# Attention outputs as two matmuls per block, one per head, summed by VectorE

## The chip, the cores and the metric

The kernel runs on one core of a Trainium2 chip. The metric is the device time of one execution in microseconds (us), the median over several runs. Besides the times there is one profiled execution, whose trace gives the start and the duration of every instruction on each engine.

## The reference

Attention over 8 batches, 8 heads, 576 positions and head size 64, in fp32, each query seeing 32 keys (heads 0 to 3: the last 32; heads 4 to 7: every fourth of the last 128). Behind it stands a gated feed-forward layer on the 4608 tokens.

```
scores = scale * q @ k^T, masked;  attn = softmax(scores);  x = attn @ v
xn  = x / sqrt(mean(x*x) + 1e-6) * rms_g
out = (silu(xn @ w_gate) * (xn @ w_val)) @ w_out        # 512 -> 1536 -> 512
```

## The kernel before

The tokens are cut into 16 units of 288. Heads go in pairs, four pairs c = 0 to 3 for each unit. A pair's queries are cut into blocks: three blocks of 96 queries for c < 2 (keys: 96 or 128 rows) and four blocks of 72 queries for c >= 2 (72 keys in even units, 104 in odd ones). That makes 14 blocks for a unit.

Products that need fp32 are made from two parts, a high one rounded to the type fp32r and a low one that is the rest; three of the four cross products are kept. In the feed-forward layer each product is three matmuls of 128x128 weights against 288 columns (`three`, lines 653 and 656). Attention does the same from the fourth unit on (u >= NEX = 3; the three units before use plain fp32).

Everything is issued by one hand-written schedule in slots. Slot after slot, the feed-forward layer of unit u takes, for j = 0 to 11, a gate slot (`gate`: 12 matmuls into `g`), a value slot (`val`, into `v`) and a projection slot (`proj` of the j before, into four accumulators `acc`). The attention of unit u+1 is fitted in between: behind the feed-forward matmuls of every second slot comes an attention event (`attend`, `products`). In the steady state an event holds, on TensorE in this order, the output matmuls of one block (o), two transposes of a later block's probabilities (t) and two score matmuls of a still later block (s). Events fall in turn on a projection, a value and a gate slot. In the text they are called P, V and G events. A unit has 36 slots: in 28 of them every second one has an event with scores, and the same holds for transposes and outputs, each shifted.

Work on the other engines is put off with `later(dt, rank, fn)`: it is issued dt slots later, sorted by rank, at the start of that slot (`flush`), before the slot's matmuls. Each engine runs its own instructions strictly in this order. For VectorE (DVE in the profile) the order behind an event in slot n is:

- behind a P event, slot n+1: `low_part` (line 469, at once behind ScalarE's copy `pt`, line 467), then `scores_max` (lines 379 and 384); slot n+2: `scores_norm` of an older block (404, 405), `add` (442), `silu` (698, reads `g` out of PSUM)
- behind a V event, slot n+1: `prod` (711, reads `v` out of PSUM), `scores_max`; slot n+2: `scores_norm`, `add`, `low_part`
- behind a G event, slot n+1: `silu`, `scores_max`; slot n+2: `low_part`, `scores_norm`, `add`, `prod`

PSUM has two banks, `g` and `v`, that gate and value products take in turn (`bank`). A projection slot's transposes, and those of a value slot in units from the fourth on, go into a tile of their own in bank `g` of the j that runs. So the transposes of a V event can start only when `silu` has read that bank; and the next gate product can start only when `prod` has read the value product. The outputs of an event have one bank, `o`.

For a block's outputs both heads' values stand side by side as 128 weight columns: `vhi` (ScalarE, line 319) and `vlo` (GpSimd, line 323). One matmul takes `vhi` against high and low probabilities of both heads (line 500: 4 x 96 or 4 x 72 columns), one takes `vlo` against the high ones (line 501), into the same place. Of each result only the half of the rows that belongs to the head is used. `take` (ScalarE, line 431) copies the low probabilities' part to `xraw`, and one slot later `add` (VectorE, line 442) adds the other part out of PSUM.

Of the kernel before, what the change touches and what calls it, by code (L numbers as in the profile page):

```python
# [11 lines left out]
F32R = mybir.dt.float32r  # L12
U32 = mybir.dt.uint32
AF = mybir.ActivationFunctionType
ALU = mybir.AluOpType
PSUM = bass.MemoryType.PSUM

B, H, S, D = 8, 8, 576, 64
DM, FF = 512, 1536
NT = B * S  # L20
P = 128
# [3 lines left out]
DIL = 4  # L25
QB = 96
NC = DM // P
NJ = FF // P
NNAT = 2
NEX = 3  # L30
# [31 lines left out]
def geometry(u, c):  # L62


    half = u % 2
    if c < NC // 2:
        if half:
            return [(QB * i, QB * i, 0, P) for i in range(U // QB)], QB, U + W
        return [(QB * i, max(QB * i - W, 0), 0 if i else W, P if i else QB)
                for i in range(U // QB)], QB, U  # L70
    nq = U // DIL
    keys = nq + (W if half else 0)
    return [(nq * r, keys * r, 0 if half else W, keys) for r in range(DIL)], nq, keys * DIL
# [3 lines left out]
def attn_moe(ctx: ExitStack, tc: tile.TileContext, qk_in, v_in, w_gate, w_val, w_out, rms_g, outT):  # L77
# [4 lines left out]
    V, A, G, PE = nc.vector, nc.scalar, nc.gpsimd, nc.tensor  # L82
# [36 lines left out]
    def later(dt, rank, fn):  # L119
        put_off.setdefault(now[0] + dt, []).append((rank, fn))  # L120
# [134 lines left out]
    heads, vs, late = {}, {}, []  # L255
# [39 lines left out]
    def load_v(b):  # L295

        if b is not None and b[0] >= NNAT:
            u, c, i = b
            vt = sb.tile([P, 2, D], F32, tag="vt", name=f"vt_{u}_{c}_{i}", bufs=3)
            nc.sync.dma_start(out=vt.rearrange("p a d -> p (a d)"), in_=v_in[u, c][:, i * 2 * D:(i + 1) * 2 * D])  # L300
            vs[b] = vt

    def further(b, n):

        k = everything.index(b) + n
        return everything[k] if k < len(everything) else None
# [4 lines left out]
    vparts = {}  # L311

    def split_v(b, dt):
        k = everything.index(b) % 2

        def hi():
            if k not in vparts:
                vparts[k] = [late[0].tile([P, 2, D], F32R, name=f"v{p}_{k}", bufs=1) for p in ("hi", "lo")]
            A.copy(out=vparts[k][0], in_=vs[b])  # L319

        def lo():
            vh, vl = vparts[k]
            G.tensor_tensor(out=vl, in0=vs.pop(b), in1=vh, op=ALU.subtract)  # L323
            load_v(further(b, 3))

        later(dt, 3.3, hi)
        later(dt, 5.1, lo)

    def after(u, h, n):

        k = u * H + h + n
        return divmod(k, H) if k < NU * H else None
# [37 lines left out]
    st, xraw, xsq = {}, {}, {}  # L370
# [44 lines left out]
    def take(u, c, i, o):  # L415

        blocks, nq, _ = geometry(u, c)
        if (u, c) not in xraw:
            xraw[u, c] = sb.tile([P, U], F32, tag="xraw", name=f"xraw_{u}_{c}", bufs=NC)
        x = xraw[u, c]  # L420
        if c < NC // 2:
            to = x[:, QB * i:QB * i + nq]
        else:
            to = x.rearrange("p (j r) -> p r j", r=DIL)[:, i, :]
        copy = V.tensor_copy if i % 2 and u == 0 and c == NC - 1 else A.copy
        if u < NEX:
            for a in range(2):
                copy(out=to[a * D:(a + 1) * D], in_=o[a * D:(a + 1) * D, a * nq:(a + 1) * nq])
        else:
            for a in range(2):  # L430
                A.copy(out=to[a * D:(a + 1) * D], in_=o[a * D:(a + 1) * D, (2 + a) * nq:(3 + a) * nq])  # L431
        if i == len(blocks) - 1:
            dt = 1 if c != 1 or u < NEX else 4
            later(dt, 0.44 if u >= NEX and (now[0] + dt - ends) % 3 == 0 else 2.5 if u else 1.9, lambda: square(u, c))

    def add(u, c, i, o):
        _, nq, _ = geometry(u, c)
        x = xraw[u, c]
        to = x[:, QB * i:QB * i + nq] if c < NC // 2 else x.rearrange("p (j r) -> p r j", r=DIL)[:, i, :]
        for a in range(2):  # L440
            rows = slice(a * D, (a + 1) * D)
            V.tensor_tensor(out=to[rows], in0=o[rows, a * nq:(a + 1) * nq], in1=to[rows], op=ALU.add)  # L442

    def square(u, c):
        first = c == 0
# [10 lines left out]
    def bursts(u):  # L456
        return [(u, c, i) for c in range(NC) for i in range(len(geometry(u, c)[0]))]

    everything = [b for u in range(NU) for b in bursts(u)]
# [14 lines left out]
    def products(q, t, o, t_ps, s_tag="s", o_tag="o", wait=0):  # L474


        if q:
            s_ps = ps.tile([P, 512], F32, tag=s_tag, name=f"s_{q[0]}_{q[1]}_{q[2]}")
        if o:
            o_ps = ps.tile([P, 512], F32, tag=o_tag, name=f"o_{o[0]}_{o[1]}_{o[2]}")  # L480
            pt = st.pop(o)
        if t:
            p, _ = st.pop(t)
        def transposed(a):
            blocks, nq, _ = geometry(*t[:2])
            n = blocks[t[2]][3]
            PE.transpose(t_ps[:n, a * QB:a * QB + nq], p[:nq, a, :n], ident[:nq, :nq])  # L487

        def output(a):
            blocks, nq, _ = geometry(*o[:2])  # L490
            n = blocks[o[2]][3]
            if a:
                return
            out = o_ps[:, :2 * nq].rearrange("d (a q) -> d a q", a=2)
            if o[0] < NEX:
                PE.matmul(out, vs.pop(o)[:n].rearrange("k a d -> k (a d)"), pt[:n, 0, :, :nq], start=True, stop=True)
                return
            vh, vl = (part[:n].rearrange("k a d -> k (a d)") for part in vparts[everything.index(o) % 2])
            both = o_ps[:, :4 * nq].rearrange("d (t a q) -> d t a q", t=2, a=2)
            PE.matmul(both, vh, pt[:n, :, :, :nq], start=True, stop=False)  # L500
            PE.matmul(out, vl, pt[:n, 0, :, :nq], start=False, stop=True)  # L501

        def scored(a):
            blocks, nq, _ = geometry(*q[:2])
            qc, kc, _, n = blocks[q[2]]
            sv = s_ps[:QB].rearrange("q (a t k) -> q a t k", a=2, t=2)
            if q[0] < NEX:
                qk = heads[q[0], 2 * q[1] + a]
                PE.matmul(sv[:nq, a, 0, :n], qk[:, qc:qc + nq], qk[:, U + kc:U + kc + n], start=True, stop=True)  # L509
                return  # L510
            qs, ks = heads[q[0], 2 * q[1] + a]
            PE.matmul(sv[:nq, a, :, :n], qs[:, qc:qc + nq], ks[:, :, kc:kc + n], start=True, stop=True)  # L512

        order = ((t, transposed), (o, output), (q, scored))
        if t and t[0] >= NEX:
            order = ((o, output), (t, transposed), (q, scored))
        parts = [(b, fn, a) for b, fn in order for a in range(2)]
        for b, fn, a in parts:
            if b:
                fn(a)  # L520
        if t:
            later(1, 0.2, lambda: untranspose(t, t_ps, wait))
        if o:
            later(1, 0.5, lambda: take(*o, o_ps))
            if o[0] >= NEX:
                later(2, -0.3, lambda: add(*o, o_ps))
            if o[0] < NEX:
                later(1, 9, lambda: load_v(further(o, 3)))
            far = further(o, 2)
            if far and far[0] >= NEX:  # L530
                split_v(far, 8 if o[0] < NEX else 1)
        if q:
            later(1, 0.7, lambda: scores_max(*q, s_ps))
            later(2, 0.42 if wait == 1 else 2, lambda: scores_exp(*q))
            later(3 if q[0] < NNAT else 4, -1, lambda: scores_norm(*q))
            u, c, i = q
            nxt = after(u, 2 * c, 2)
            nb = len(geometry(u, c)[0])
            if u < NEX:
                if u == NNAT - 1 and c == NC - 1 and i == nb - 1:  # L540
                    for h in range(4):
                        later(1, 9, lambda h=h: load(NNAT, h))
                if u >= NNAT and i == nb - 1 and c < NC - 1:
                    for a in range(2):
                        later(1, 9, lambda a=a: load(*after(u, 2 * c + a, 4)))
                if u == NEX - 1 and c == NC - 1 and i == nb - 1:
                    for a in range(2):
                        later(3 + a, 9, lambda a=a: split(NEX, a, (1, 2, 2, 3), G, G))
            elif nxt and i == 0:
                split(*nxt, (1, 2, 2, 3), G, G)  # L550
                split(nxt[0], nxt[1] + 1, (2, 3, 3, 4) if c < NC - 1 else (1, 2, 3, 4), G, G)
# [274 lines left out]
    for u in range(NU):  # L826
        for j in range(NJ):
            for part in range(0 if u + j else 2, 3):
                t = 3 * (u * NJ + j) + part
# [95 lines left out]
```

## Time and profile before

| what | value |
|---|---|
| median of 3 runs | 1115.47 us (1114.78 to 1117.87) |
| the profiled execution | 1115.13 us, span 1113.3 us, granted TensorE clock 1.0 |
| TensorE busy | 1101.7 us, 99% of the span |
| VectorE busy | 671.8 us, 60% |
| ScalarE (ACT) busy | 708.8 us, 64% |
| GpSimd (POOL) busy | 673.2 us, 60% |
| DMA engines | 24.1% of the span in the main queue |

A row of the timeline reads: start in us from the beginning of the span, duration, engine, line of the kernel, operation, tile written and tiles read, shape and count (x2 when two like instructions are merged), and in brackets the idle time of the engine before it and what ended it. A row of the groups reads: line, engine, operation, shapes, count, then total busy us and the mean in ns of one, then idle time before. PE is TensorE's matmul, PEld its weight load. Matmuls overlap, so what one costs is read from the distance of two starts and not from its duration.

### The profile page before, as it was taken

How to read it: one execution, taken by the hardware profiler on the slowest of the kernel's cores; microseconds unless marked ns; L12 is line 12 of the kernel's file. 1: busy time of each engine (PE TensorE's matmuls, PEld its weight loads, DVE VectorE, ACT ScalarE, POOL GpSimd, SP SyncE). 2: the span in 40 equal slices, each digit the busy share in tenths (PEclk: the TensorE clock that was granted, in tenths of full speed). 3: DMA queues.
4: the chain of work that ended last, by engine and by line, in shares of the span. 5: the costliest groups of instructions: out<-in, count | busy, mean ns of one | idle time of the engine just before them, and what ended most of it. 6: DMA issues, size and time to landing. Idle time of an engine off the chain costs nothing.

```text
span 1113.3 us, 25463 instructions
## 1 busy us (share of the span) xinstructions
PE 1101.7 (99%) x8362; PEld 1077.5 (97%) x8362; DVE 671.8 (60%) x2734; ACT 708.8 (64%) x2579; POOL 673.2 (60%) x1154
## 2 busy tenths in 40 slices
PE   8899999999999999999999999999999999999998
PEld 6787999999999999999999999999999999999998
DVE  6989667656565565656656565665656656565312
ACT  7795676757576675767657576675757657575311
POOL 6423588656586675757657575675658657584211
PEclk9999999999999999999999999999999999999999
DMA  9665212212131131311212121131212212120000
GB/s 255 194 245 183 74 47 82 84 35 81 41 94 50 42 86 40 95 39 57 80 39 84 42 83 54 48 96 28 88 43 80 64 32 80 49 78 13 11 12 22
DMA packets 61543, 82.16 MB, mean 74 GB/s; under 512 B 7299, under 2 KB 41091, under 8 KB 61411
## 3 DMA queue, kind: packets, MB, share of 16 engines
q1 hardware_dynamic: 61410, 80.54, 24.1%
q8 instruction: 66, 1.08, 0.4%
q14 instruction: 67, 0.54, 0.2%
HBM read 71.08 MB, written 9.44 MB: 72 GB/s over the span
## 4 chain that ended last, share of the span: by engine, by line
PE 95%; DVE 1%; DMA 1%; ACT 1%; POOL 1%; issue 0%; SPq 0%; POOLq 0%; DVEq 0%; ACTq 0%
PE acc L656 17%; PE g L656 17%; PE v L656 17%; PE acc L653 9%; PE g L653 9%; PE v L653 9%; PE s L512 3%; PE o L500 2%; PE acc L650 2%; PE v L650 2%; PE g L650 2%; PE t L487 2%; PE o L501 1%; PE g L487 1%; DMA v<-in_v_dram 1%; PE s L509 1%
## 5 line engine op out<-in xcount | busy, mean ns | idle before, releaser
L723 POOL TENSOR_TENSOR hlo<-th,hhi 128x288 fp32r<-128x288 f32 x179 | 145.8, 814 | 185.2 <-ACT hhi L722 168.1
L656 PE MATMUL acc<-hhi,lo 128*128 128x288 f32 x720 | 212.7, 295 | 0.0
L698 DVE SCALAR_TENSOR_TENSOR th<-th,g 128x288 f32<-128x288 f32 x180 | 81.8, 454 | 212.5 <-ACT pt L467 130.6
L395 ACT ACTIVATE t<-t,sum 96x128 f32<-96x128 f32 (+3 forms) x448 | 165.3, 372 | 33.0 <-DVE sum L384 31.6
L656 PE MATMUL g<-xhi,lo 128*128 128x288 f32 x612 | 180.3, 295 | 0.0
L656 PE MATMUL v<-xhi,lo 128*128 128x288 f32 x612 | 180.2, 294 | 0.0
L693 ACT ACTIVATE th<-g 128x288 f32<-128x288 f32 x180 | 73.9, 410 | 151.4 <-PE g L487 57.7
L411 POOL TENSOR_SCALAR t<-t,sum 72x72 f32<-72x72 f32 (+3 forms) x414 | 149.9, 374 | 32.2 <-DVE sum L405 20.0
L323 POOL TENSOR_TENSOR vlo<-vt,vhi 128x128 fp32r<-128x128 f32 x182 | 84.2, 463 | 116.6 <-ACT vhi L319 113.5
L656 PEld LDWEIGHTS acc<-hhi,lo 128*128 128x128 f32 x720 | 135.4, 188 | 0.0
L722 ACT CAST hhi<-th 128x288 fp32r<-128x288 f32 x180 | 77.8, 432 | 85.3 <-DVE th L711 84.7
L442 DVE TENSOR_TENSOR xraw<-o,xraw 64x72 f32<-64x72 f32 (+1 forms) x364 | 97.2, 267 | 42.1 <-ACT xraw L431 38.6
L656 PEld LDWEIGHTS v<-xhi,lo 128*128 128x128 f32 x612 | 115.1, 188 | 0.0
L656 PEld LDWEIGHTS g<-xhi,lo 128*128 128x128 f32 x612 | 115.1, 188 | 0.0
L711 DVE TENSOR_TENSOR th<-th,v 128x288 f32<-128x288 f32 x180 | 81.0, 450 | 54.7 <-PE v L656 53.0
L653 PE MATMUL acc<-hhi,hi_o 128*128 128x288 f32 x360 | 109.0, 303 | 0.0
L653 PE MATMUL g<-xhi,hi_g 128*128 128x288 f32 x357 | 106.8, 299 | 0.0
L656 PE MATMUL acc<-hlo,hi_o 128*128 128x288 f32 x360 | 106.4, 296 | 0.0
L431 ACT COPY xraw<-o 64x72 f32<-64x72 f32 (+1 forms) x364 | 95.4, 262 | 9.8 <-PE o L501 7.7
L353 POOL TENSOR_TENSOR ks<-qk,ks 128x288 fp32r<-128x288 f32 (+2 forms) x104 | 93.3, 902 | 3.1
L656 PE MATMUL g<-xlo,hi_g 128*128 128x288 f32 x322 | 95.1, 295 | 0.0
L362 POOL TENSOR_TENSOR qs<-qk,qs 64x288 fp32r<-64x288 f32 x104 | 84.2, 809 | 14.7 <-ACT qs L357 7.8
(188 smaller groups left out, 3524.5 us busy)
## 6 DMA issues: line engine op xcount, KB each, us to landing
qk<-in_qk_dram SPq DMA_DIRECT2D x60, 288.0 KB, 2.8
vt<-in_v_dram SPq DMA_DIRECT2D x196, 64.0 KB, 1.9
qk<-in_qk_dram SPq DMA_DIRECT2D x30, 352.0 KB, 3.1
out_dram<-ot SPq DMA_DIRECT2D x64, 144.0 KB, 1.9
qk<-in_qk_dram SPq DMA_DIRECT2D x30, 304.0 KB, 2.8
raw<-in_w_gate_dram SPq DMA_DIRECT2D x12, 512.0 KB, 4.7
raw<-in_w_val_dram SPq DMA_DIRECT2D x12, 512.0 KB, 4.2
raw<-in_w_out_dram SPq DMA_DIRECT2D x12, 512.0 KB, 4.3
```

What stands on the lines that cost most here:

```text
L323: G.tensor_tensor(out=vl, in0=vs.pop(b), in1=vh, op=ALU.subtract)
L353: ek.tensor_tensor(out=ks[:, 1, :nkt], in0=kr, in1=ks[:, 0, :nkt], op=ALU.subtract)
L362: eq.tensor_tensor(out=qs[D:], in0=qr[D:], in1=qs[D:], op=ALU.subtract)
L395: A.activation(out=t[:nq, a, :n], in_=t[:nq, a, :n], func=AF.Exp, scale=-1.0, bias=sm[:nq, a, 0:1], accum_out=sm[:nq, a, 1:2] if u or i % ...
L411: (V if u == 0 and (c, i) > (NC - 1, 0) else G).tensor_scalar(out=t[:nq, a, :n], in0=t[:nq, a, :n], scalar1=sm[:nq, a, 3:4], scalar2=1.0, ...
L431: A.copy(out=to[a * D:(a + 1) * D], in_=o[a * D:(a + 1) * D, (2 + a) * nq:(3 + a) * nq])
L442: V.tensor_tensor(out=to[rows], in0=o[rows, a * nq:(a + 1) * nq], in1=to[rows], op=ALU.add)
L653: PE.matmul(out, wh[:, cc, :], xh, start=start, stop=False)
L656: PE.matmul(out, w[:, cc, :], v, start=False, stop=stop and k == 1)
L698: V.scalar_tensor_tensor(out=t, in0=t, scalar=1.0, in1=g, op0=ALU.add, op1=ALU.mult)
L711: V.tensor_tensor(out=t, in0=t, in1=v_ps[:, :U], op=ALU.mult)
L723: (V if (u, j) == (NU - 1, NJ - 1) else G).tensor_tensor(out=lo, in0=t, in1=hi, op=ALU.subtract)
```

## The change

From the fourth unit on a head's high and low values stand side by side as one weight of 128 columns. There is one matmul for each head, against that head's high and low probabilities (2 x 96 or 2 x 72 columns). Rows 0 to 63 of the result then hold the high values' products with both parts, rows 64 to 127 the low values' products. VectorE adds three of the four quarters: a `tensor_reduce` over the two parts of rows 0 to 63, written to `xraw`, and an add of rows 64 to 127's product with the high part. ScalarE's two copies and the separate `add` one slot later are gone; `take` keeps its slot, with rank 0.55 instead of 0.5, so all four VectorE instructions of a block stand behind `low_part` and ahead of `silu` and `scores_max` of that slot.

```diff
 def split_v(b, dt):  # hi(), lo()
-                vparts[k] = [late[0].tile([P, 2, D], F32R, name=f"v{p}_{k}", bufs=1) for p in ("hi", "lo")]
-            A.copy(out=vparts[k][0], in_=vs[b])
+                vparts[k] = late[0].tile([P, 2, 2, D], F32R, name=f"vhl_{k}", bufs=1)
+            A.copy(out=vparts[k][:, :, 0], in_=vs[b])
...
-            vh, vl = vparts[k]
-            G.tensor_tensor(out=vl, in0=vs.pop(b), in1=vh, op=ALU.subtract)
+            vp = vparts[k]
+            G.tensor_tensor(out=vp[:, :, 1], in0=vs.pop(b), in1=vp[:, :, 0], op=ALU.subtract)
...
 def take(u, c, i, o):
-                A.copy(out=to[a * D:(a + 1) * D], in_=o[a * D:(a + 1) * D, (2 + a) * nq:(3 + a) * nq])
+                ours, cols = to[a * D:(a + 1) * D], 2 * a * nq
+                V.tensor_reduce(out=ours, in_=o[:D, cols:cols + 2 * nq].rearrange("d (t q) -> d q t", t=2),
+                                axis=mybir.AxisListType.X, op=ALU.add)
+                V.tensor_tensor(out=ours, in0=o[D:, cols:cols + nq], in1=ours, op=ALU.add)
...
-    def add(u, c, i, o):
-        ...
-            V.tensor_tensor(out=to[rows], in0=o[rows, a * nq:(a + 1) * nq], in1=to[rows], op=ALU.add)
...
 def output(a):
-            PE.matmul(both, vh, pt[:n, :, :, :nq], start=True, stop=False)
-            PE.matmul(out, vl, pt[:n, 0, :, :nq], start=False, stop=True)
+            vp = vparts[everything.index(o) % 2]
+            PE.matmul(o_ps[:, 2 * a * nq:2 * (a + 1) * nq].rearrange("d (t q) -> d t q", t=2),
+                      vp[:n, a].rearrange("k t d -> k (t d)"), pt[:n, :, a, :nq], start=True, stop=True)
...
-            later(1, 0.5, lambda: take(*o, o_ps))
-            if o[0] >= NEX:
-                later(2, -0.3, lambda: add(*o, o_ps))
+            later(1, 0.5 if o[0] < NEX else 0.55, lambda: take(*o, o_ps))
```

More of the change, by code (lines that the diff above doesn't have):

```diff
@@ L434, in take @@
             later(dt, 0.44 if u >= NEX and (now[0] + dt - ends) % 3 == 0 else 2.5 if u else 1.9, lambda: square(u, c))
-    def add(u, c, i, o):
[L437 to L442, printed above, removed]
     def square(u, c):
@@ L491, in output @@
             n = blocks[o[2]][3]
-            if a:
-                return
-            out = o_ps[:, :2 * nq].rearrange("d (a q) -> d a q", a=2)
             if o[0] < NEX:
+                if a:
+                    return
+                out = o_ps[:, :2 * nq].rearrange("d (a q) -> d a q", a=2)
                 PE.matmul(out, vs.pop(o)[:n].rearrange("k a d -> k (a d)"), pt[:n, 0, :, :nq], start=True, stop=True)
                 return
[L498 to L501, printed above, removed]
+            vp = vparts[everything.index(o) % 2]
+            PE.matmul(o_ps[:, 2 * a * nq:2 * (a + 1) * nq].rearrange("d (t q) -> d t q", t=2),
+                      vp[:n, a].rearrange("k t d -> k (t d)"), pt[:n, :, a, :nq], start=True, stop=True)
         def scored(a):
```

## The prediction

> **What bounds the kernel now.** I read the page's busy shares first, then the chain that ended last, then starts in the timeline.
>
> ```profile
> span 1113.3 us, 25463 instructions
> PE 1101.7 (99%) x8362; PEld 1077.5 (97%) x8362; DVE 671.8 (60%) x2734; ACT 708.8 (64%) x2579; POOL 673.2 (60%) x1154
> ...
> PE 95%; DVE 1%; DMA 1%; ACT 1%; POOL 1%; issue 0%; SPq 0%; POOLq 0%; DVEq 0%; ACTq 0%
> ```
>
> TensorE is busy for 99% of the span and is 95% of the chain. So time taken off TensorE counts at once, as long as nobody makes it wait; time added to VectorE counts only where TensorE waits for it. VectorE's 60% says nothing of that: its work stands in a fixed order with deadlines, and I look at these.
>
> **TensorE's part.** Distances of starts give what a matmul costs. First an event that holds outputs alone, then the outputs of a block of 96 queries:
>
> ```profile
> 498.55 0.30 PE L500 MATMUL o<-pt,vhi 104*128 104x288 f32 x1
> 498.69 0.23 PE L501 MATMUL o<-pt,vlo 104*128 104x144 f32 x1
> 498.75 0.34 PE L653 MATMUL g<-xhi,hi_g 128*128 128x288 f32 x1
> 498.93 0.29 PE L656 MATMUL g<-spare,hi_g 128*128 128x288 f32 x1
> 499.06 0.30 PE L656 MATMUL g<-xhi,lo 128*128 128x288 f32 x1
> ...
> 457.60 0.34 PE L500 MATMUL o<-pt,vhi 128*128 128x384 f32 x1
> 457.77 0.25 PE L501 MATMUL o<-pt,vlo 128*128 128x192 f32 x1
> 457.86 0.33 PE L487 MATMUL t<-ident,t 96*128 96x96 f32 x2
> ```
>
> 288 columns cost 0.13 us (498.93 to 499.06), 384 cost 0.17, 192 cost 0.09, so about 0.46 ns for a column. Were that all, the new pair would cost twice the old second matmul: 0.09 less for a block of 96 queries, 0.07 less for one of 72 (144 columns, 498.69 to 498.75). But from the start at 498.69 to that of the second matmul behind it (498.93) pass 0.24 us, not 0.07 + 0.13. The 144-column matmul takes 0.11 us when 128 weight columns must be loaded behind it. So I read 0.11 as the least between two matmuls when the second one's weight has 128 columns. The weight loads' groups agree:
>
> ```profile
> L501 PEld LDWEIGHTS o<-pt,vlo 128*128 128x128 f32 x66 | 12.4, 188 | 0.0
> ...
> L501 PEld LDWEIGHTS o<-pt,vlo 72*128 72x128 f32 x48 | 9.1, 190 | 0.0
> ```
>
> A load of 128 columns takes 188 to 190 ns with 128 rows or 72, so the short key blocks get no cheaper loads. The change keeps two loads of 128 columns for a block, and its first matmul (192 or 144 columns, 0.09 or 0.07 us) is now too short to cover the second load. It costs 0.112 (the 0.24 less a spacing of 0.13, with the third decimal that many spacings give). The second new matmul has the old second one's columns and successor, so nothing changes there. What is saved is the old first matmul less 0.112: 0.177 - 0.112 = 0.065 us for the 78 blocks of 96 queries (13 units x 6), 0.133 - 0.112 = 0.021 for the 104 of 72. That is 5.1 + 2.2 = 7.3 us. The ends are nothing (less can't be: no column and no load is added) and the column count's 13.7 (78 x 0.088 + 104 x 0.066); I take 7.3, as the event of 498.55 has the same load behind the same columns.
>
> On the page "TensorE: Matmul & The Clock Gate", section "LDWEIGHTS (loading the stationary operand)", the Trainium skill speaks against the larger gain: a load takes its columns over 1.2 in ns, whatever the rows. For 128 columns that is 107 ns; the trace agrees with its 0.11. By the page the sum would be 78 x 0.070 + 104 x 0.026 = 8.2 us.
>
> **What else moves at no cost.** ScalarE loses two copies a block; it isn't on the chain, and its `pt` and `hhi` wait for others. The high and low values are written as 64-column pieces instead of whole rows, the same elements in the same places of both queues; DMAs and SP's order stay. `take` waits on VectorE for the second output matmul. Queued behind it are `silu` and `scores_max`; whoever waits for these is what follows.
>
> **VectorE's part.** How long are the four instructions?
>
> ```profile
> L403 DVE TENSOR_REDUCE sum<-t 72x2 f32<-72x144 f32 x4 | 1.2, 297 | 0.7 <-ACT t L395 0.7
> ...
> L403 DVE TENSOR_REDUCE sum<-t 96x2 f32<-96x192 f32 x2 | 0.7, 345 | 0.0
> ...
> 455.04 0.34 DVE L469 TENSOR_TENSOR pt<-t,pt 128x192 fp32r<-128x192 f32 x1
> 455.31 0.41 DVE L379 TENSOR_TENSOR t<-s,mask 96x256 f32<-96x256 f32 x1
> ...
> 456.36 0.17 DVE L405 RECIPROCAL sum<-sum 96x2 f32<-96x2 f32 x1
> 456.44 0.50 DVE L442 TENSOR_TENSOR xraw<-o,xraw 64x96 f32<-64x96 f32 x2
> 456.98 0.46 DVE L698 SCALAR_TENSOR_TENSOR th<-th,g 128x288 f32<-128x288 f32 x1
> ```
>
> The reduces read 192 or 144 elements, as these rows do (0.345 and 0.297 us, from SBUF and to two outputs; the new ones read PSUM and write 96 or 72). An add is 0.25 (half of 0.50); I add 0.03 where 72 queries are written with a stride. Independent instructions overlap: L379 starts 0.07 before L469 ends, L442 0.09 before L405 ends. Behind the adds nothing does: L698 starts 0.04 after them. An add also needs its reduce's result. So I give each step from the first add to the one behind the last a gap of 0.03: 0.35 + 0.03 + 0.26 + 0.02 + 0.35 + 0.03 + 0.26 + 0.03 = 1.33; with 72 queries 0.33 and 0.29 give about the same. I take 1.32 as the shift of what follows. Low end: a reduce as short as an add and no gaps, 1.0. High end: 0.06 more for a reduce of many short sums, as much as 60 elements more at the rate of these two rows ((0.345 - 0.297) over 48), 1.45.
>
> The Trainium skill, page "VectorE: DVE Perf Modes", section "Two Vector instructions with no wait between them", has a rule for the gaps: an instruction is held until the one before is done if an input or the output starts in another quadrant of 32 partitions than before. The trace agrees (the 0.04 at 456.98); by the rule every step of the new `take` behind its first reduce is held.
>
> Now the deadlines. Behind a P event VectorE's order becomes low part, four new ones, `scores_max`, norm, `silu`; the old adds went behind the norm. In the rows above (unit of 457.86) L379 moves from 455.31 to 456.63, L405 ends at 457.85 instead of 456.53, and `silu` may overlap it: 457.77 instead of 456.98, which is +0.79. It ends at 458.23. The V event's transposes (457.86) wait for that bank. They would come at 457.73, since the outputs of the P event and of this V event are 0.065 shorter each. With 0.04 for the handing over TensorE waits 0.54 us. The same place in other units and blocks:
>
> ```profile
> 523.32 0.45 DVE L698 SCALAR_TENSOR_TENSOR th<-th,g 128x288 f32<-128x288 f32 x1
> 524.48 0.33 PE L487 MATMUL t<-ident,t 96*96 96x96 f32 x2
> ...
> 479.85 0.45 DVE L698 SCALAR_TENSOR_TENSOR th<-th,g 128x288 f32<-128x288 f32 x1
> 480.62 0.29 PE L487 MATMUL t<-ident,t 72*104 72x72 f32 x2
> ...
> 545.98 0.46 DVE L698 SCALAR_TENSOR_TENSOR th<-th,g 128x288 f32<-128x288 f32 x1
> 546.94 0.23 PE L487 MATMUL t<-ident,t 72*72 72x72 f32 x1
> ...
> 468.21 0.45 DVE L698 SCALAR_TENSOR_TENSOR th<-th,g 128x288 f32<-128x288 f32 x1
> 469.38 0.29 PE L487 MATMUL t<-ident,t 72*104 72x72 f32 x2
> ```
>
> - first such V event, even units (524.48): margin 0.71 instead of 0.42, wait 0.25
> - third, odd units (480.62): +0.73 (the strided adds taken out are 0.06 longer), and 0.13 earlier by the G event (below); margin 0.32, events 0.04 shorter, 0.04 to hand over: wait 0.36. Even units (546.94), margin 0.50: 0.18
> - second, odd units (469.38): margin 0.72, +0.79, 0.13 earlier, 0.13 and 0.04 as at 457.86: 0.11; in even units, and at the other two V events of a unit, `silu` waits for ScalarE today, which covers the shift
>
> Behind a G event VectorE is idle today:
>
> ```profile
> 472.90 0.34 PE L500 MATMUL o<-pt,vhi 128*128 128x384 f32 x1
> ...
> 474.23 0.46 DVE L698 SCALAR_TENSOR_TENSOR th<-th,g 128x288 f32<-128x288 f32 x1 [2.43 <-ACT pt L467]
> ```
>
> The second output matmul ends 0.42 us behind the start of the first (457.60 to 457.77 + 0.25); 0.065 less and 0.04 for the handing over make 0.40. So the four run from 473.30 to 474.63, and `silu` is 0.40 late. The adds that stood ahead of `prod` are gone, 0.54 (456.44 to 456.98). `prod` comes about 0.13 earlier, and with it `hhi`, `pt` and the next low part. Behind V events nothing but `scores_max` and older work waits, and its bank is asked for two slots later.
>
> Sum of waits, 7 odd and 6 even units (the last odd one without the 0.36, since `silu` is done earlier where no next unit is scored): 7 x (0.54 + 0.11) + 6 x 0.36 + 6 x (0.25 + 0.18) = 9.3 us. Against 7.3 saved: +2.0. The profiled execution took 1115.13 us (1.8 more than its span), 0.34 below the median; 1115.13 + 2.0 = 1117.1.
>
> **The rivals.**
>
> *The new VectorE chain is shorter* (faster). Were the four 1.13 us (a reduce like an add, 0.25), each wait falls by 0.19 where it is that long: 7 x 0.35 + 6 x 0.17 + 6 x 0.06 = 3.8 us, and the time is 1115.1 - 7.3 + 3.8 = 1111.6; at 1.0 some 1.7 us of waits are left: 1109.5. For it: the rows of reduces are of two long sums, not 96 short ones. Against: 192 elements took 0.345.
>
> *`silu` behind P events decides* (slower). Each 0.1 us more in the four costs 32 waits, 3.2 us. It passes 0.3% from 0.04 us beyond my 1.33; at 1.45 the time is 1117.1 + 3.8 = 1120.9. For it: margins of 0.32 to 0.72. Against: nothing in the rows asks for longer reduces.
>
> *The second load hides after all* (columns alone count): 13.7 saved, but the deadlines come 0.05 to 0.09 earlier at 32 places, so waits are 11.3: 1112.7. Against: the 0.24 at 498.69.
>
> *The waits don't arise*, because low parts come sooner once ScalarE has less to do: 1115.1 - 7.3 = 1107.8. For it: two instructions less on ScalarE in each event. Against: its copies stood behind `pt`.
>
> **How the numbers follow.** A measurement of this kernel can tell about 0.3% (3.3 us) from no change. My sum stands (gain and waits about cancel, 1112 to 1119): 0.40, with the third rival in it. Shorter chain or no waits: 0.28. `silu` decides: 0.32. So faster 0.28, same 0.40, slower 0.32. The range takes in the ends of the take's length and leaves some of both tails: 1109 to 1122.
>
> **What would show it.** Right: in events the two output matmuls 0.11 apart; four VectorE instructions of some 1.3 us behind the low part; `silu` ending just before a V event's transposes, and there a gap of 0.2 to 0.5 us on TensorE three times in an odd unit, twice in an even one; some 144 us more on VectorE (182 blocks x (1.33 - 0.54)), and ScalarE's two copies a block gone. Wrong: outputs 0.09 or 0.07 apart, reduces well off 0.3 us, gaps elsewhere (gate products waiting for `prod`, scores for `scores_max`), or no gaps.

## The result

| | median us | ratio to the kernel before (95% interval) |
|---|---|---|
| before | 1115.24 (4 runs) | |
| after | 1121.93 (1121.88 to 1124.24, 4 runs) | 1.0058 [1.0046, 1.0070] |

The change makes the kernel 6.7 us slower. The forecast was 1117.1, +2.0 us.

The profiled execution of the kernel after took 1124.24 us. That is 2.3 us above the median, and it was already 2.7 us behind the kernel before where the changed units begin: its granted clock (the column PEclk, behind the five engines) was 0.95 and 0.94 in the first 60 us, where the kernel before had 1.00.

```profile
core 0: us, PE busy (x) PEld busy (x) DVE busy (x) ACT busy (x) POOL busy (x), PEclk, DMA share, GB/s
0.00:30.00 30.00, 24.75 (x144) 18.95 (x145) 19.69 (x106) 20.87 (x81) 19.58 (x53) 0.95 0.96 245
30.00:60.00 30.00, 27.86 (x139) 22.30 (x139) 27.68 (x81) 21.44 (x73) 12.83 (x14) 0.94 0.58 182
```

From the first changed unit (at 190 us) to the last slot the two traces differ by 5.7 us. That is what has to be explained; the rest of the 6.7 is not placed (the profiled execution ran 0.7 us longer behind its last instruction).

The page of the kernel after, busy shares and the chain that ended last:

```profile
PE 1105.5 (98%) x8362; PEld 1074.1 (96%) x8362; DVE 782.8 (70%) x3098; ACT 618.8 (55%) x2215; POOL 671.7 (60%) x1154
...
PE 76%; DVE 12%; ACT 5%; POOL 3%; issue 2%; DMA 1%; SPq 0%; DVEq 0%; POOLq 0%; ACTq 0%
```

TensorE's share of the chain fell from 95% to 76%; VectorE now holds 12%, ScalarE 5% and GpSimd 3%. So TensorE waits, and not for VectorE alone. The view of waits names two places (engine, line, what it waited for; us in all, times, longest). Neither stands in the same view of the kernel before, beyond one wait of 0.4 us for `rd`:

```profile
PE t L482 <- DVE th L690: 2.6, 7, 0.5
...
PE bps L594 <- ACT rd L578: 1.6, 7, 0.4
```

This view counts only idle time beyond the modelled ends of matmuls, so its sums are too small. I measured the waits by the distance from the first feed-forward matmul of a slot to that of the next, slot by slot in both traces, summed over the 13 changed units:

| slot (what stands behind its feed-forward matmuls) | after minus before, us | one unit: odd / even |
|---|---|---|
| events where nobody waits, blocks of 96 queries | -0.77 to -0.90 for each of four | -0.06 to -0.07 (mean) |
| events where nobody waits, blocks of 72 queries | -0.20 to -0.34 for each of seven | -0.01 to -0.03 |
| first V event of a unit | +4.89 | +0.48 to 0.62 / +0.17 to 0.22 |
| third V event | +2.00 | +0.26 / +0.06 |
| second V event | +0.26 | +0.08 / -0.04 |
| gate slot with the spread of the root mean square (`bps`) | +3.53 | +0.26 to 0.35 in 12 units |

What the two new output matmuls cost shows an event that holds outputs alone, with the same instructions behind it as the event of 498.55 in the prediction. Two windows are put together, so that the two like instructions aren't merged into one row:

```profile
503.56 0.23 PE L494 MATMUL o<-pt,vhl 104*128 104x144 f32 x1
...
503.63 0.28 PE L494 MATMUL o<-pt,vhl 104*128 104x144 f32 x1
503.74 0.34 PE L645 MATMUL g<-xhi,hi_g 128*128 128x288 f32 x1
503.92 0.29 PE L648 MATMUL g<-spare,hi_g 128*128 128x288 f32 x1
```

The second starts 0.07 behind the first and the instruction behind it another 0.11 later, where the kernel before had 0.14 and 0.06 (498.55, 498.69, 498.75). Over all events where nobody waits the two distances are 0.07 and 0.11 for 72 queries, 0.09 and 0.11 to 0.12 for 96.

The groups of `take`, with its different shapes apart:

```profile
L432 DVE TENSOR_REDUCE xraw<-o 64x72 f32<-64x144 f32 x208 | 62.3, 299 | 52.2 <-PE o L494 50.8
L434 DVE TENSOR_TENSOR xraw<-o,xraw 64x72 f32<-64x72 f32 x208 | 60.5, 291 | 7.1
...
L432 DVE TENSOR_REDUCE xraw<-o 64x96 f32<-64x192 f32 x156 | 54.1, 347 | 15.9 <-PE o L494 14.7
L434 DVE TENSOR_TENSOR xraw<-o,xraw 64x96 f32<-64x96 f32 x156 | 40.4, 259 | 5.4
```

And the place that the prediction worked through, a P event followed by the first V event of an odd unit, in the timeline of the kernel after:

```profile
458.94 0.76 DVE L626 TENSOR_TENSOR xlo<-xraw,xhi 128x288 fp32r<-128x288 f32 x1 [0.83 <-ACT xhi L625]
...
459.62 0.35 DVE L464 TENSOR_TENSOR pt<-t,pt 128x192 fp32r<-128x192 f32 x1
...
459.89 0.34 DVE L432 TENSOR_REDUCE xraw<-o 64x96 f32<-64x192 f32 x1
...
460.26 0.26 DVE L434 TENSOR_TENSOR xraw<-o,xraw 64x96 f32<-64x96 f32 x1
...
460.53 0.35 DVE L432 TENSOR_REDUCE xraw<-o 64x96 f32<-64x192 f32 x1
...
460.92 0.26 DVE L434 TENSOR_TENSOR xraw<-o,xraw 64x96 f32<-64x96 f32 x1
...
461.21 0.42 DVE L379 TENSOR_TENSOR t<-s,mask 96x256 f32<-96x256 f32 x1
...
462.09 0.15 DVE L404 TENSOR_REDUCE sum<-sum 96x2 f32<-96x4 f32 x1
...
462.13 0.36 PE L494 MATMUL o<-pt,vhl 128*128 128x192 f32 x2
...
462.36 0.43 DVE L690 SCALAR_TENSOR_TENSOR th<-th,g 128x288 f32<-128x288 f32 x1
...
462.84 0.39 PE L482 MATMUL t<-ident,t 96*128 96x96 f32 x2 [0.35 <-DVE th L690]
```

From the first reduce (459.89) to the instruction behind the last add (461.21) pass 1.32 us. `silu` ends at 462.79, the transposes start at 462.84, 0.71 us behind the outputs. Without a wait it is 0.20 (458.26 to 458.46 in the kernel with three moves, below).

### The profile page after: what moved, and what is told of

The parts are those of the page before. It is cut to its first block, busy times and chain, and to the rows that moved or that the text cites. A ratio compares the mean times of both kernels' runs of the same rounds, so it can differ in the third digit from the quotient of the medians.

```text
span 1122.5 us, 25515 instructions
## 1 busy us (share of the span) xinstructions
PE 1105.5 (98%) x8362; PEld 1074.1 (96%) x8362; DVE 782.8 (70%) x3098; ACT 618.8 (55%) x2215; POOL 671.7 (60%) x1154
## 4 chain that ended last, share of the span: by engine, by line
PE 76%; DVE 12%; ACT 5%; POOL 3%; issue 2%; DMA 1%; SPq 0%; DVEq 0%; POOLq 0%; ACTq 0%
PE acc L648 14%; PE g L648 14%; PE v L648 12%; PE acc L645 7%; PE g L645 7%; PE v L645 6%; PE o L494 2%; PE acc L642 2%; DVE t L384 2%; PE s L506 2%; PE v L642 2%; PE t L482 2%; PE g L642 2%; DVE th L690 2%; DVE xraw L432 2%
## 5 line engine op out<-in xcount | busy, mean ns | idle before, releaser
L395 ACT ACTIVATE t<-t,sum 96x128 f32<-96x128 f32 (+3 forms) x448 | 166.1, 373 | 125.0 <-DVE sum L384 123.4
L685 ACT ACTIVATE th<-g 128x288 f32<-128x288 f32 x180 | 73.6, 409 | 184.4 <-PE g L648 92.6
L432 DVE TENSOR_REDUCE xraw<-o 64x72 f32<-64x144 f32 (+1 forms) x364 | 116.3, 320 | 68.1 <-PE o L494 65.6
L323 POOL TENSOR_TENSOR vhl<-vt,vhl 128x128 fp32r<-128x128 f32 x182 | 84.2, 463 | 72.7 <-ACT vhl L319 69.8
L434 DVE TENSOR_TENSOR xraw<-o,xraw 64x72 f32<-64x72 f32 (+1 forms) x364 | 100.9, 277 | 12.5
```

The lines of the kernel that those rows point to most:

```text
L323: G.tensor_tensor(out=vp[:, :, 1], in0=vs.pop(b), in1=vp[:, :, 0], op=ALU.subtract)
L395: A.activation(out=t[:nq, a, :n], in_=t[:nq, a, :n], func=AF.Exp, scale=-1.0, bias=sm[:nq, a, 0:1], accum_out=sm[:nq, a, 1:2] if u or i % ...
L432: V.tensor_reduce(out=ours, in_=o[:D, cols:cols + 2 * nq].rearrange("d (t q) -> d q t", t=2), axis=mybir.AxisListType.X, op=ALU.add)
L434: V.tensor_tensor(out=ours, in0=o[D:, cols:cols + nq], in1=ours, op=ALU.add)
```

## The experiments

Each was timed 4 to 11 times beside the kernel before, whose medians were 1116.09 us for the first four and 1116.47 for the last four. By its ratio the kernel after would have some 1122.7 there. "Slots" is the difference to before from the first changed unit on, measured as above.

**The matmuls alone.** ScalarE copies one quarter and VectorE's `add`, at its old place, adds the low values' quarter; the high values' product with the low probabilities is left out.

```diff
-                V.tensor_reduce(out=ours, in_=o[:D, cols:cols + 2 * nq].rearrange("d (t q) -> d q t", t=2), ...)
-                V.tensor_tensor(out=ours, in0=o[D:, cols:cols + nq], in1=ours, op=ALU.add)
+                A.copy(out=to[a * D:(a + 1) * D], in_=o[:D, 2 * a * nq:(2 * a + 1) * nq])
...
-            later(1, 0.5 if o[0] < NEX else 0.55, lambda: take(*o, o_ps))
+            later(1, 0.5, lambda: take(*o, o_ps))
+            if o[0] >= NEX:
+                later(2, -0.3, lambda: add(*o, o_ps))
```

> The new matmuls alone: one per head with high and low values as one weight, but ScalarE copies one quarter of the sum and VectorE adds one, in the slots of the kernel before. The product of high values and low probabilities is left out of the sum, so that the evictions are those of before in number, size and place. Theory (a 128-column weight load sets 0.11 us as the least of the first matmul): TensorE gains 0.065 us in 78 blocks and 0.021 in 104, nobody waits longer, 7.3 us faster than before: 1107.9. Rival 1 (columns alone count): 13.7 us faster, 1101.5. Rival 2 (the gain is lost elsewhere on TensorE, the whole slowdown of the change is from its matmuls): 1115 or more.

Measured: 1111.40 us, ratio 0.9962 [0.9948, 0.9975]; slots -4.8 instead of -7.3. A miss by some 2.5 us. The saving of a matmul pair is exact where nobody waits (-0.06 to -0.07 and -0.02 to -0.03 an event). Where it is lost, the rows of before and of this kernel show a common cause. First before, then the matmuls alone:

```profile
487.03 0.57 DVE L442 TENSOR_TENSOR xraw<-o,xraw 64x72 f32<-64x72 f32 x2
...
487.59 0.19 PEld L656 LDWEIGHTS acc<-hhi,lo 128*128 128x128 f32 x1
487.73 0.19 PEld L500 LDWEIGHTS o<-pt,vhi 104*128 104x128 f32 x1
```

```profile
485.29 0.59 DVE L442 TENSOR_TENSOR xraw<-o,xraw 64x72 f32<-64x72 f32 x2
...
485.75 0.19 PEld L655 LDWEIGHTS acc<-hhi,lo 128*128 128x128 f32 x1
485.99 0.30 PEld L499 LDWEIGHTS o<-pt,vhl 104*128 104x128 f32 x2
```

The old `add` gives the outputs' bank free, and the next event's first output load wants it. Before, that load starts 0.14 behind the one ahead of it, TensorE's own spacing, and 0.13 behind the add's end: there was hardly any slack. With the matmuls shorter TensorE arrives earlier, and the load starts 0.24 behind the one ahead, 0.11 behind the add's end (485.88). The trace settles how much this makes: in 33 of the 182 events the first output load starts 0.115 to 0.117 behind the add's end, in all others at least 0.16. In these 33 the load's distance to the one ahead grew by 2.4 us in sum against before, nearly the whole miss. In the change itself the bank is read one slot earlier, so this wait does not arise: in the kernel with three moves the smallest distance is 0.78.

**VectorE's part alone.** The kernel before with its matmuls; VectorE does a reduce and an add for each head, at the new place. The add takes in one part a second time.

```diff
-                A.copy(out=to[a * D:(a + 1) * D], in_=o[a * D:(a + 1) * D, (2 + a) * nq:(3 + a) * nq])
+                V.tensor_reduce(out=ours, in_=o[rows, :4 * nq].rearrange("d (t a q) -> d a q t", t=2, a=2)[:, a], ...)
+                V.tensor_tensor(out=ours, in0=o[rows, a * nq:(a + 1) * nq], in1=ours, op=ALU.add)
...
-            later(1, 0.5, lambda: take(*o, o_ps))
-            if o[0] >= NEX:
-                later(2, -0.3, lambda: add(*o, o_ps))
+            later(1, 0.5 if o[0] < NEX else 0.55, lambda: take(*o, o_ps))
```

> The matmuls of before, but VectorE alone takes the outputs out, with a reduce and an add a head of the new sizes at the new place (the add adds one part a second time, for its time alone). Theory (the waits come from VectorE's longer turn; savings on TensorE only bring the deadlines nearer by 0.13 or 0.04 us): TensorE waits about 0.44 and 0.14 us at the first V event of odd and even units, 0.24 and 0.05 at the third, none at the second, and 0.27 a unit where the norm's factors are spread: 9 us slower than before, 1124. Rival (the new matmuls and the longer turn only hurt together): 1115 to 1117.

Measured: 1127.87 us, ratio 1.0101 [1.0087, 1.0114]; slots +9.7 in the profiled execution, the fastest of its four: first V event +4.1, third +1.9, second +0.6 (none was expected there), spread +3.5. The waits belong to VectorE's part and stand at the same four places without the new matmuls.

**The take behind the score maximum, behind V events.** This tests the cause of the 3.5 us that the prediction did not have. Rows of the kernel before around the last V event of a unit with scores:

```profile
435.36 0.45 DVE L711 TENSOR_TENSOR th<-th,v 128x288 f32<-128x288 f32 x1 [0.63 <-PE v L656]
...
436.70 0.08 DVE L384 DVE_READ_ACCUMULATOR2_ANT sum<- 96x1 f32 x1
...
437.36 0.40 ACT L395 ACTIVATE t<-t,sum 96x128 f32<-96x128 f32 x1
...
439.72 0.45 DVE L698 SCALAR_TENSOR_TENSOR th<-th,g 128x288 f32<-128x288 f32 x1 [0.57 <-ACT th L693]
...
443.79 0.91 ACT L586 ACTIVATE rd<-ident,rst_lo 96x96 fp32r<-96x96 f32 x3 [1.65 <-POOL rst_lo L574]
...
444.56 0.58 PE L602 MATMUL bps<-rd,ones 96*128 96x288 f32 x2
```

The same place in the kernel after:

```profile
439.64 0.45 DVE L703 TENSOR_TENSOR th<-th,v 128x288 f32<-128x288 f32 x1 [0.63 <-PE v L648]
440.01 0.29 DVE L432 TENSOR_REDUCE xraw<-o 64x72 f32<-64x144 f32 x1
...
442.08 0.40 ACT L395 ACTIVATE t<-t,sum 96x128 f32<-96x128 f32 x1 [0.96 <-DVE sum L384]
442.18 0.08 DVE L384 DVE_READ_ACCUMULATOR2_ANT sum<- 96x1 f32 x1
...
442.87 0.43 ACT L443 ACTIVATE sq<-xraw 128x288 f32<-128x288 f32 x1
...
443.88 0.40 ACT L685 ACTIVATE th<-g 128x288 f32<-128x288 f32 x1
444.32 0.46 DVE L690 SCALAR_TENSOR_TENSOR th<-th,g 128x288 f32<-128x288 f32 x1 [0.53 <-ACT th L685]
...
448.38 0.91 ACT L578 ACTIVATE rd<-ident,rst_lo 96x96 fp32r<-96x96 f32 x3 [1.65 <-POOL rst_lo L566]
...
448.85 0.30 PE L594 MATMUL bps<-rd,ones 96*128 96x288 f32 x1
...
449.33 0.40 PE L594 MATMUL bps<-rd,ones 96*128 96x288 f32 x1 [0.19 <-ACT rd L578]
```

Count from `prod` (435.36 and 439.64). The second maximum comes at +1.34 before and +2.54 after, the exponentials (L395) at +2.00 and +2.44, `silu` at +4.36 and +4.68, ScalarE's `rd` (the factors that the two `bps` matmuls spread over the rows) at +8.43 and +8.74. The maximum is 1.2 us later; 0.4 of it reaches ScalarE, where squares, copies and the gate's tanh (L685) stand behind the exponentials in order; `silu`, VectorE's work on the next block's scores behind it, the root on GpSimd and `rd` pass 0.3 of it on, and the two `bps` matmuls wait. ScalarE's idle time ahead of the exponentials shows the same over the whole span (before, then after; the last field):

```profile
L395 ACT ACTIVATE t<-t,sum 96x128 f32<-96x128 f32 (+3 forms) x448 | 165.3, 372 | 33.0 <-DVE sum L384 31.6
```

```profile
L395 ACT ACTIVATE t<-t,sum 96x128 f32<-96x128 f32 (+3 forms) x448 | 166.1, 373 | 125.0 <-DVE sum L384 123.4
```

```diff
-            later(1, 0.5 if o[0] < NEX else 0.55, lambda: take(*o, o_ps))
+            later(1, 0.5 if o[0] < NEX else 0.75 if wait == 2 else 0.55, lambda: take(*o, o_ps))
```

> The changed kernel, but behind V events the take stands behind scores_max (rank 0.75 instead of 0.55). Theory (behind the last V event of a unit ScalarE's exponentials wait for scores_max, which waits for the take; the square, two copies and tanh stand behind them on ScalarE, then silu, prod and the norm's root: the norm's factors come 0.27 to 0.35 us late, 3.5 us in all): that wait goes, the ones at V events' transposes stay, 3.5 us faster than the changed kernel: 1118.4. Rival (the square behind the take sets that chain, which the take's end alone decides): the wait stays or grows, 1121.9 or more.

Measured: 1117.73 us, ratio 1.0012 [1.0003, 1.0021]. The spread's slot went from +3.5 to -1.0, and the V events kept theirs (+4.9, +2.2, +0.4). Confirmed.

**The low part behind the take, behind P events.** Ahead of the low part VectorE may wait for ScalarE's `pt`; the take needs only the outputs, which are there sooner, so placed first it could fill that wait.

```diff
-            later(1, 0.4 if wait > 1 else -1.5, low_part) if wait else low_part()
+            if wait:
+                later(1, 0.4 if wait > 1 else -1.5, low_part)
+            else:
+                low_parts[b] = low_part
...
+            if t[0] >= NEX and not wait:
+                later(1, 0.58, lambda: low_parts.pop(t)())
```

> The changed kernel, but behind P events the low part (line 464) is issued behind the four VectorE instructions that take the outputs out, not ahead of them. They can then run while VectorE waits for the probabilities' copy. Theory (silu behind P events sets the waits at V events): at the second and third V event of a unit VectorE had 0.8 to 1.1 us of idle time ahead of the low part, which hides most of the take, so these waits (about 1.1 and 2.3 us in all) go; at the first V event the low part stands behind line 626's subtraction, VectorE has no idle time between, and the wait of 0.57 and 0.27 us stays; so does the one at the norm's factors. 3.4 us faster than the changed kernel: 1118.5. Rival (the length of VectorE's turn as such counts, wherever it stands): 1121.9.

Measured: 1128.21 us, ratio 1.0106 [1.0092, 1.0120]. A miss: 1118.5 was expected. The first and third V events' waits did go (+4.9 to +0.5, +2.0 to +0.5), but a larger one came elsewhere. The waits and the timeline of this kernel:

```profile
PE v L650 <- DVE pt L464: 7.3, 13, 1.0
```

```profile
460.30 0.36 DVE L464 TENSOR_TENSOR pt<-t,pt 128x192 fp32r<-128x192 f32 x1
...
460.71 0.40 PE L650 MATMUL v<-xhi,hi_g 128*128 128x288 f32 x1 [0.67 <-DVE pt L464]
```

A P event's transposes lie in a bank that the next value product takes, and the low part reads them there. Its place at once behind `pt` gives that bank free in time. Moved, it cost 9.4 us in the gate slot ahead of the first V event (1.2 in the first changed unit, then 0.8 in odd units and 0.5 in even ones) and 2.4 in two more slots. The first V event's wait went only because TensorE had lost as much one slot before: there another operation (`xlo`, 458.94 above) covers the wait for `pt`, and nothing is left to fill.

**The same for one event of a unit**, the one ahead of the third V event (output index 6).

```diff
+            elif behind:
+                low_parts[b] = low_part
...
+            behind = t[0] >= NEX and not wait and o and everything.index(o) % 14 == 6
...
+            if behind:
+                later(1, 0.58, lambda: low_parts.pop(t)())
```

> The changed kernel with the low part of the probabilities behind the take at one of the unit's events only, the one in the projection slot ahead of the unit's third value event. Theory: the third wait alone goes (2.2 us), and no value product waits for the low part as it did in the first gate slot when all of them were moved: about 1120.5 where the changed kernel has 1122.7. Rival (every low part that is moved delays the value product that takes its bank): about 1123 to 1124.

Measured: 1120.74 us, ratio 1.0044 [1.0030, 1.0057]. The third V event went from +2.0 to +0.5, and no value product waits. Confirmed: there the take fills a wait, and the low part still ends 0.07 to 0.13 us ahead of the value product that takes its bank (0.70 to 0.79 in the kernel after; 0.055 at the value products that wait in the run above). So it is in time, but hardly.

**The norm's scale behind `silu`.** At the start of a V event's slot `scores_norm` stands ahead of `silu`, so it adds 0.27 us (462.09 to 462.36 above) to the 1.3 of the take.

```diff
-            later(3 if q[0] < NNAT else 4, -1, lambda: scores_norm(*q))
+            later(3 if q[0] < NNAT else 4, 0.65 if q[0] >= NEX and wait == 1 else -1, lambda: scores_norm(*q))
```

> The changed kernel with one move: at the gate slots where an output head is taken behind a value slot, VectorE scales the norm (scores_norm) behind silu instead of ahead of it. Theory (silu is late at the value slots because the 1.3 us of take and the norm's scale stand ahead of it): silu comes 0.34 us earlier, so the first value wait of a unit falls from 0.57 (odd) and 0.27 (even) to 0.23 and 0, the second and third to 0; 7 x 0.34 + 6 x 0.27 + about 2.2 for the third = -6.5 to -7 us against the changed kernel, while the 3.5 us at the gate slot with the root mean square's spread stay. About 1115.7 where the kernel before has 1116.1. Rival (the scale that is now later holds GpSimd's and the next slot's work instead): no gain, about 1122.7.

Measured: 1115.22 us, ratio 0.9992 [0.9983, 1.0001]. First V event +4.9 to +1.5 (odd +0.26, even -0.05, some 0.26 less in each), second and third waits to nothing, the spread's 3.6 us unchanged. Confirmed, with the 0.27 of the rows and not the 0.34 that was expected.

**Three moves.** The take behind the score maximum, the scale behind `silu`, and the last of the next unit's input parts (`part(3)`, rank 0.6 to 0.45) ahead of the gate's parts.

```diff
-            later(1, 0.5 if o[0] < NEX else 0.55, lambda: take(*o, o_ps))
+            later(1, 0.5 if o[0] < NEX else 0.75 if wait == 2 else 0.55, lambda: take(*o, o_ps))
...
-            later(3 if q[0] < NNAT else 4, -1, lambda: scores_norm(*q))
+            later(3 if q[0] < NNAT else 4, 0.65 if q[0] >= NEX and wait == 1 else -1, lambda: scores_norm(*q))
...
-                later((2, 3, 4, 5)[c], 0.6, lambda c=c: part(c))
+                later((2, 3, 4, 5)[c], 0.6 if c < 3 else 0.45, lambda c=c: part(c))
```

> The changed kernel with three moves in VectorE's order: the output head's take behind the score maximum at value slots, the norm's scale behind silu, and the last quarter of the normalized input's two parts ahead of the gate's high and low parts. Theory: the silu waits (7.2 us) and the wait for the spread (3.5 us) are both gone; of the 7.3 us that the matmuls save, some 2.5 go to other waits, as in the kernel with the matmuls alone (4.7 left). So 1109 to 1111.5 where the kernel before has 1116.1. Rival (TensorE then waits for the next late operation on VectorE, which has the same 1.3 us more in each output slot): 1114 to 1117.

Measured: 1109.18 us, ratio 0.9939 [0.9926, 0.9953], 0.6% below the kernel before. Its chain, and the place of 462.84 above:

```profile
PE 94%; POOL 2%; ACT 1%; DVE 1%; DMA 1%; issue 1%; SPq 0%; POOLq 0%; DVEq 0%; ACTq 0%
```

```profile
455.39 0.36 DVE L464 TENSOR_TENSOR pt<-t,pt 128x192 fp32r<-128x192 f32 x1 [0.52 <-ACT pt L462]
...
457.87 0.45 DVE L690 SCALAR_TENSOR_TENSOR th<-th,g 128x288 f32<-128x288 f32 x1
...
458.26 0.37 PE L494 MATMUL o<-pt,vhl 128*128 128x192 f32 x2
...
458.46 0.33 PE L482 MATMUL t<-ident,t 96*128 96x96 f32 x2
```

The low part waits for `pt` alone, no longer for `xlo`, and comes 2.87 us ahead of the outputs instead of 2.51. `silu` ends 0.14 us before the transposes, which start 0.20 behind the outputs. Slots: -7.3, of which 6.6 in slots with outputs and 1.0 at the spread, where the kernel before had waited a little; other slots lost 0.3. The 2.5 us that were expected to go to other waits did not, since the wait for the old add doesn't arise here. How the three moves share the gain wasn't taken apart further.

**The order on the kernel before.** The last two of the moves (scale and `part(3)`) without the change; the diff is the last four lines above, put on the kernel before:

> Control: the kernel before with the norm's scale behind silu and the last quarter of the input's parts ahead of the gate's parts, nothing else changed. Theory: nothing waits for silu in the kernel before, so the order makes no difference: 1116.1 within 0.3%. Rival (the moves are worth something without the change): 1112 to 1114, and then the gain of the kernel with three moves is not the change's.

Measured: 1117.49 us, ratio 1.0007 [0.9997, 1.0017]; no slot differs. So the order is worth nothing where nothing waits; with it the change itself is worth 6.8 us (0.0061 x 1116.5).

## Why the prediction was right in part

Right, with sizes:

- *TensorE's saving.* -0.065 and -0.021 an event were predicted; -0.064 and -0.020 came on average where nobody waits, which makes 7.1 us for 182 blocks. Columns alone would have given -0.088 and -0.066, so that rival falls. The place was read wrongly: the two output matmuls start 0.09 or 0.07 apart, which the prediction had named as a sign of being wrong, and the 0.11 stands behind the second one (503.63 to 503.74). In the event of 498.55 too the extra time stands one spacing behind the short matmul (498.75 to 498.93). A pair costs the same by either reading, 0.20 and 0.18. By the page "TensorE: Matmul & The Clock Gate", section "LDWEIGHTS (loading the stationary operand)", of the Trainium skill the sum was 8.2 us; the 7.1 is nearer to the rows' 7.3.
- *The take.* 1.33 us predicted, 1.32 in the rows. The single gaps are 0.01 to 0.04: each of the four starts only when the one before is done. That agrees with the rule that the prediction cites from the Trainium skill, page "VectorE: DVE Perf Modes", section "Two Vector instructions with no wait between them". Reduces of many short sums took as long as the rows of two long ones (347 and 299 ns against 345 and 297), so the rivals with a shorter or longer chain fall. VectorE's busy time grew by 111 us (671.8 to 782.8) and not by 144: the four groups hold 217.3 us where the old add's two held 97.2, and the gaps, which the 1.33 has in it, aren't busy time.
- *`silu` at the V events.* Predicted 0.54 and 0.25 for the first, 0.36 and 0.18 for the third, 0.11 and 0 for the second. Measured, with the event's own saving added: about 0.59 and 0.27, 0.28 and 0.09, 0.14 and 0.02. In sum 9.1 against 9.3; that it comes so near is partly luck, since the third event's waits were taken too long and the other two's too short.

Wrong: the step "Behind V events nothing but `scores_max` and older work waits, and its bank is asked for two slots later". It asked only when the scores' bank is wanted again, and not who reads the maximum. ScalarE's exponentials do, and behind these stand in ScalarE's order the square, the tanh for the next `silu`, and with them the chain to `bps`. The step put this wait at nothing; it is 3.5 us in 12 units, at the `bps` matmuls (a gap elsewhere, as its signs of being wrong have it), and with it 2.0 becomes 5.5; the slots show 5.7. Two kernels show it from both sides: VectorE's part alone has the 3.5, and with the take behind the maximum it is gone.

The range held the time by luck: 1121.93 lies just inside its end of 1122, because it reached to the slower rival's end. That rival had the right sign by the wrong mechanism: the take was not longer. What the prediction held most likely, a time within 0.3% of before, did not come. The rival in which no waits arise had 1107.8; the matmuls alone came to 4.7 below their before and not 7.3, and the full kernel came near it only with three moves in VectorE's and ScalarE's order.

## What to carry to other kernels

When work moves to an engine that is idle 40% of the time, list for each instruction queued behind it who reads its result, and follow that reader's own queue to the end: the 3.5 us that were overlooked here went over ScalarE and GpSimd before they reached TensorE. When a change is slower than its parts are worth, look for cheap reorderings at the places that wait: four instructions of 1.3 us an event cost 12.6 us in one order (9.1 + 3.5) and about 1 in another. And before moving an instruction, ask which buffer it gives free, since its place may be a deadline for that.

## What the runs showed of the hardware

Of two matmuls of 144 or 192 columns, each with 128 weight columns of its own, the second started 0.07 or 0.09 us behind the first, and the instruction behind it 0.11 later (503.56, 503.63, 503.74). A reduce out of PSUM took 299 ns for 64x144 into 72 sums and 347 ns for 64x192 into 96. An add that writes 72 elements with a stride of four took 291 ns, one that writes 96 side by side 259 ns. A weight load that waits for VectorE started 0.11 us behind the end of the add it waited for (485.88 to 485.99; 0.115 to 0.117 in all 33 cases of that kernel), and a matmul that waits for VectorE 0.05 us behind (460.66 to 460.71, 462.79 to 462.84). The profiled execution of the kernel after, with its granted clock of 0.94 to 0.95 in the first 60 us, reached the first changed unit 2.7 us later than the kernel before; that of the three moves, with the same mean clock of 0.997, 2.8 us later.
